# Band attention with a folded GLU: every head from 16 on transposed by VectorE and DMA, the first batch in plain fp32, and a fixed table of steps

## The chip, the cores and the metric

The kernel runs on one core of a Trainium2 chip. The metric is the time of one execution on the device in microseconds. The median of three runs of the kernel before is 893.46 us (892.77 to 895.96). Five engines run their own queues in order: TensorE (PE, with its weight loads PEld), VectorE (DVE), ScalarE (ACT), GpSimd (POOL) and SyncE (SP), which issues all DMAs here.

## The reference

Eight batches of eight heads, 512 local and 32 global tokens, 64 channels a head. Local queries see the global keys and a band of 32 local keys to each side; global queries see everything. The result goes through a bilinear GLU and two more matrices. All inputs are fp32 but the four weights, which arrive as 64-bit floats.

```python
def _attn_ref(q_l, k_l, v_l, q_g, k_g, v_g):          # B, H, Sl, D = 8, 8, 512, 64; Sg = 32
    k_all = np.concatenate([k_g, k_l], axis=2)
    v_all = np.concatenate([v_g, v_l], axis=2)
    s_g = scale * np.matmul(q_g, k_all.transpose(0, 1, 3, 2))
    out_g = np.matmul(sm(s_g), v_all)
    s_ll = scale * np.matmul(q_l, k_l.transpose(0, 1, 3, 2))
    mask = np.abs(pos[:, None] - pos[None, :]) <= 32
    s_ll = np.where(mask, s_ll, -1e9)
    s_lg = scale * np.matmul(q_l, k_g.transpose(0, 1, 3, 2))
    a_l = sm(np.concatenate([s_lg, s_ll], axis=-1))
    out_l = np.matmul(a_l, np.concatenate([v_g, v_l], axis=2))
    return np.concatenate([out_g, out_l], axis=2)

def _moe_ref(x, w1, w2, w3, w_out):                   # x: 4352 tokens x 512
    return ((x @ w1) * (x @ w2) @ w3) @ w_out
```

## The kernel before

**Precision.** Most matmuls take operands declared as `float32r`. So as to lose little precision the kernel splits an operand into a high part (a cast copy, `hi_of`, L308) and a low part (the operand minus its high part, `lo_of`, L311) and adds products of the parts. Local keys are held twice, on both halves of the partitions; of a head's queries the high part lies on one half and the low part on the other. So `kh` times both query parts and `kl` times both make four products in two instructions. P and V are split in the same way; the values come out on two halves of the partitions and are added (`values_half` copies one half to `cb`, `values_sum` adds it).

**A head** (64 of them, number n = 8 * batch + head). Loads of k, q and v; the casts and subtractions; `scores` (L386) on TensorE, four blocks of 128 queries with windows of 192 or 256 keys; `minus_max` (L398) on VectorE and `exps` (L402) on ScalarE write P into one of two tiles `Ps`; the inverse sums go through DRAM and come back spread over the partitions (`inverse_out`, `inverse_in`). P has to be transposed for the product with V. In most heads `transposes` (L448) does it with seven 128x128 transposes on TensorE into PSUM. In every second head from 16 on (`turned`, L30) `turn` (L427) transposes 32x32 blocks on VectorE, `turned_out` (L433) writes the blocks to DRAM and two edges within SBUF with six DMAs, and `turned_in` (L442) fetches them with two DMAs. In both cases `weights_hi` and `weights_lo` then write the parts of P transposed into `PTh`, `PTl` and `G` (global keys), from PSUM or from the P tile. There are six or seven such pieces a head: pieces 0 (own keys), 1 and 2 (the edges of the band), 3 and 6 (global keys), 4 and 5 (the global queries' weights). `values` (L506) multiplies; after two heads `join`, `normalize` and `convert` make the columns of x, and `join_g` adds up the outputs of the global queries in the tile `xg`.

**Global queries.** For each pair of heads `g_scores`, `g_half`, `g_minus_max`, and for each four heads `g_exps`, `g_normalize`, `g_transposes`, `g_weights`.

**Weights.** In the first stage the 64-bit words are unpacked to fp32 (`unit`), `fold` multiplies w3 by w_out once in plain fp32 (64 products of 512 columns), and the results are split (`fold_split`). Half of w1 and w2 comes in this stage, the rest (`w12s`) a little later.

**GLU.** `first` (L618) computes x times w1 and w2 for a quarter of the hidden units and 256 tokens, `gate_a` and `gate_b` multiply them, `second` (L647) multiplies by the folded matrix into two accumulators; after four quarters `evict` and `store`. There are 68 quarters, one for each head from head 8 on while heads last, and twelve after the last head, four of them for the global tokens.

**Order.** Everything is issued in an order that is computed while the kernel is built. Each step has a set of engines it may go to, a price on each (`COST`), a due time and the steps it needs. `list_schedule` (L129) walks through time: each engine that is free takes the available step with the earliest due time, moved by the numbers of `DUE`, `HEADS`, `UNITS` and `SUMS`. Steps that read SBUF on VectorE or GpSimd are priced as excluding each other. The engines' queues then hold the steps in the order of their starts.

## Time and profile before

| | before |
|---|---|
| median of 3 runs | 893.46 us (892.77 to 895.96) |
| profiled execution, its own time | 898.31 us |
| its span, first to last instruction | 896.5 us |
| mean granted TensorE clock | 0.978 |
| busy: PE, DVE, ACT, POOL | 832.8, 630.3, 616.4, 491.2 us |
| DMA: moved, mean rate | 103.38 MB, 115 GB/s |
| recorded DMA issues | 651, all from SP |

The page shows one execution. Its busy times are sums over the span; a group of instructions carries its line, engine, operation, tiles, shapes and count, then its busy time and the mean of one in ns, then the idle time of the engine before them and what ended it. Matmuls are pipelined, so their durations overlap and the time from one start to the next is the cost. In a table of waits the columns are the total in us, how often, and the longest. Heads can be counted by `u<-av,cb`, two for each head.

### The profile page before, as it was taken

Reading aid. Unit: us, or ns where it says so; the run is one execution under the profiler, and the core shown is the slowest. Engines: PE = TensorE matmul, PEld = TensorE weight load, DVE = VectorE, ACT = ScalarE, POOL = GpSimd, SP = SyncE. Lnnn points to the kernel's source line nnn. Section 1 sums busy time; section 2 is a strip of 40 time slices with the busy share of each in tenths; the row PEclk is TensorE's granted clock in tenths of the full one; section 3 lists DMA queues with packets and bytes.
Section 4 is the critical chain, followed back from the end, with each engine's and each line's share of the span. In section 5 each row is a group of like instructions: output and inputs, shape, how many; then the busy total and the mean of one; then the engine's idle time right before and its main releaser. Section 6 shows DMA issues by size and latency. Waiting matters only on the chain. (4 is left out here: it accounts for less than half of the span.)

```text
span 896.5 us, 17912 instructions
## 1 busy us (share of the span) xinstructions
PE 832.8 (93%) x5848; PEld 753.6 (84%) x5848; DVE 630.3 (70%) x1623; ACT 616.4 (69%) x1671; POOL 491.2 (55%) x592
## 2 busy tenths in 40 slices
PE   2788975999999999999999999999999999999995
PEld 1444645999989999999899989999999899999994
DVE  4888797888877878877787777778877798422111
ACT  4888777788878778787778777778777777312111
POOL 3455666566575767676668565857685656300000
PEclk9999876999999999999999999999999999999998
DMA  8786534424344435344535353436343522200000
GB/s 282 230 248 207 173 115 136 122 74 111 89 109 127 130 106 146 107 127 108 143 99 134 100 152 90 125 101 163 91 129 101 148 72 67 55 25 1 24 24 24
DMA packets 76917, 103.38 MB, mean 115 GB/s; under 512 B 20120, under 2 KB 38040, under 8 KB 76824
## 3 DMA queue, kind: packets, MB, share of 16 engines
q1 hardware_dynamic: 76824, 102.24, 40.8%
q8 instruction: 46, 0.75, 0.4%
q14 instruction: 47, 0.39, 0.2%
HBM read 84.71 MB, written 16.91 MB: 113 GB/s over the span
## 5 line engine op out<-in xcount | busy, mean ns | idle before, releaser
L627 PE MATMUL ap<-x,w12h 128*128 128x256 f32 x544 | 152.5, 280 | 2.1 <-ACT as__2970 L633 1.1
L627 PE MATMUL bp<-x,w12h 128*128 128x256 f32 x544 | 153.8, 283 | 0.0
L628 PE MATMUL bp<-x,w12h 128*128 128x256 f32 x544 | 152.0, 279 | 0.0
L629 PE MATMUL bp<-x,w12l 128*128 128x256 f32 x544 | 151.7, 279 | 0.0
L628 PE MATMUL ap<-x,w12h 128*128 128x256 f32 x544 | 151.0, 278 | 0.0
L629 PE MATMUL ap<-x,w12l 128*128 128x256 f32 x544 | 150.9, 277 | 0.0
L311 POOL TENSOR_TENSOR qs<-qr,qs 64x512 fp32r<-64x512 f32 x62 | 82.2, 1325 | 83.1 <-ACT qs L308 68.7
L403 ACT ACTIVATE P<-P,mn 128x192 f32<-128x192 f32 (+1 forms) x256 | 121.0, 474 | 2.8 <-DVE mn L399 1.9
L627 PEld LDWEIGHTS ap<-x,w12h 128*128 128x128 f32 x544 | 102.5, 188 | 4.1 <-ACT as__2970 L633 1.5
L628 PEld LDWEIGHTS bp<-x,w12h 128*128 128x128 f32 x544 | 103.2, 190 | 2.5
L627 PEld LDWEIGHTS bp<-x,w12h 128*128 128x128 f32 x544 | 103.3, 190 | 2.4
L628 PEld LDWEIGHTS ap<-x,w12h 128*128 128x128 f32 x544 | 102.3, 188 | 1.3 <-POOL x L311 0.2
L629 PEld LDWEIGHTS bp<-x,w12l 128*128 128x128 f32 x544 | 103.0, 189 | 0.0
L629 PEld LDWEIGHTS ap<-x,w12l 128*128 128x128 f32 x544 | 102.2, 188 | 0.0
L399 DVE CUSTOM_DVE_ANT_0 P<-s,cs 128x192 f32<-128x192 f32 (+1 forms) x256 | 86.9, 387 | 13.1 <-PE s L395 11.0
L532 DVE TENSOR_TENSOR u<-av,cb 64x352 f32<-64x352 f32 x128 | 65.0, 518 | 28.3 <-ACT cb L308 25.8
L308 ACT COPY cb<-av 64x352 f32<-64x352 f32 x127 | 56.6, 447 | 38.6 <-PE av L518 36.8
L395 PE MATMUL s<-kh,qs 128*128 128x192 f32 (+1 forms) x256 | 66.6, 292 | 17.0 <-DVE mg L569 7.0
L311 POOL TENSOR_TENSOR kl<-kr,kh 128x608 fp32r<-128x608 f32 x49 | 74.8, 1526 | 12.6 <-ACT kh L308 9.4
L764 PE MATMUL w<-wo,w3f 128*128 128x512 f32 x128 | 63.7, 645 | 10.8 <-DVE w3f L688 10.8
L395 PEld LDWEIGHTS s<-kh,qs 128*128 128x128 f32 x256 | 51.2, 200 | 22.4 <-DVE mg L569 8.8
L518 PE MATMUL av<-PTl,vs 128*128 128x192 f32 (+1 forms) x256 | 65.3, 280 | 3.9 <-DVE PTl L311 3.9
(800 smaller groups left out, 2399.7 us busy)
## 6 DMA issues: line engine op xcount, KB each, us to landing
kr<-in_kd_t_dram SPq DMA_DIRECT2D x128, 152.0 KB, 2.9
raw_w<-in_w_t_dram SPq DMA_DIRECT2D x24, 512.0 KB, 5.3
kpr<-in_kp_t_dram SPq DMA_DIRECT2D x32, 272.0 KB, 3.1
out_dram<-o SPq DMA_DIRECT2D x34, 256.0 KB, 3.0
vr<-in_v_t_dram SPq DMA_DIRECT2D x32, 256.0 KB, 2.9
qr<-in_q_t_dram SPq DMA_DIRECT2D x32, 256.0 KB, 3.5
R<-rd SPq DMA_DIRECT2D x64, 128.0 KB, 3.1
pd<-P SPq DMA_DIRECT2D x96, 80.0 KB, 1.9
```

The costliest lines, as they stand in the source:

```text
L308: (nc.scalar.copy if eng in (None, nc.scalar) else eng.tensor_copy)(dst, src)
L311: (eng or nc.gpsimd).tensor_sub(dst, src, f(hi))
L395: nc.tensor.matmul(st[:, e, 0:w], qs[:, 128 * e : 128 * e + 128], kk[:, o : o + w], start=(j == e % 2 == 0), stop=(j == 1), skip_group_che ...
L399: nc.vector.tensor_tensor_reduce(blk(n, e), cut(n, T["st", n][:, e, 0 : WIN[e][1]]), cut(n, masks[e]), -0.125, 3.0e38, ALU.add, ALU.min, T ...
L403: nc.scalar.activation(blk(n, e), blk(n, e), AF.Exp, bias=T["mn", n][:, e : e + 1], scale=-1.0, accum_out=T["sm", n][:, e : e + 1])
L518: nc.tensor.matmul(av[:, o : o + c1 - c0], v, pt[:, j, c0:c1], start=False, stop=(j % 2 == y == 1), skip_group_check=True)
L532: nc.vector.tensor_add(T["u", n // 2][r : r + 64, x], T.pop(("av", n, x))[r : r + 64, 0:352], T["cb", n][r : r + 64, x])
L627: nc.tensor.matmul(d, wh[:, k, c, :], x[:, 0, 0:w], start=(k == m % 2 == 0), stop=False, skip_group_check=True)
L628: nc.tensor.matmul(d, wh[:, k, c, :], x[:, 1, 0:w], start=False, stop=False, skip_group_check=True)
L629: nc.tensor.matmul(d, wl[:, k, c, :], x[:, 0, 0:w], start=False, stop=(k == 3), skip_group_check=True)
L764: nc.tensor.matmul(T["w34", t], T["w3f", t, j // 4][:, j % 4], T["wo"][:, j], start=(j == 0), stop=(j == 7))
```

## The change

- **Turned heads.** `TURN` goes from 2 to 1: all 48 heads from 16 on are turned by VectorE and DMA, where 24 were. `NPB` = 3 tiles of P replace two.
- **xg in DRAM.** The sums of the global queries leave SBUF: after each pair of heads one small DMA (`global_out`), and four loads (`global_in`) before the last quarters.
- **First batch in plain fp32** (`FS`, `FV` = 8). For heads 0 to 7 `scores` takes q and k as loaded, 64 rows each, in one fp32 product a block; `values` takes V as loaded, 32 or 128 rows, and P's transposed parts as fp32, with the output on 64 partitions. So there are no high and low parts of k, q, v and the global v, no low parts of P, no `cb`; `values_sum` is one copy from PSUM. k is loaded once, not twice, for these heads. `PTh`, `G` and `vgs` are declared again as float32r for head 8, and four clears of them (and of `PTl`) stand after the values of head 7.
- **Order.** `list_schedule` and its numbers are gone. `in_order` reads a table: for each step its rank among all 4218, with a letter for the engine (A, D, P for ScalarE, VectorE, GpSimd) where more than one is allowed.
- **More choice of engines.** Casts and copies that only ScalarE (or ScalarE and GpSimd) made may now go to VectorE: `hi`, `xh`, `cg`, `ga` among them. By the letters, over heads 16 to 63: the four turned pieces' high parts 122 on ScalarE, 35 on VectorE, 35 on GpSimd; their low parts 104 on VectorE, 88 on GpSimd; kl 26 and 22; ql 27 and 21; cb 75 on ScalarE, 21 on VectorE.

```diff
-TURN, FROM, AHEAD = 2, 16, 6.0
+TURN, FROM, AHEAD, NPB = 1, 16, 6.0, 3
+FS, FV = 8, 8
-DUE = dict(
...
+ORDER_OF = dict(
...
+    s="34 77 105 165 242 296 334 392 460 528 634 729 836 885 923 1020 1087 1133 1177 1273 1335 1388 1427 1531 1579 "
...
+    T="1123 1165 1212 1294 1370 1417 1462 1556 1609 1644 1718 1793 1866 1912 1952 2051 2104 2137 2212 2290 2362 2405 "
...
+    dr="1151 1189 1241 1323 1401 1445 1490 1581 1635 1669 1745 1817 1893 1942 1983 2082 2135 2161 2243 2315 2389 "
...
+    kl="P378 P480 D625 P657 P760 P852 P903 P958 P1032 P1101 D1173 P1213 D1307 P1345 D1414 P1458 P1542 D1593 D1686 "
...
-def list_schedule(steps, after, held):
...
+def in_order(steps, after, held):
+    words = {k: iter(v.split()) for k, v in ORDER_OF.items()}
+    letters, out = dict(A="ACT", D="DVE", P="POOL"), []
+    for n, (key, on, *_) in enumerate(steps):
+        word = next(words[key[0]])
+        out.append((int(word.lstrip("ADP")), n, letters[word[0]] if word[0] in letters else [*on][0]))
+    out.sort()
...
-    Ps = [const.tile([128, PW], F32, tag=f"P{e}", name=f"P{e}") for e in range(2)]
+    Ps = [const.tile([128, PW], F32, tag=f"P{e}", name=f"P{e}") for e in range(NPB)]
...
-    xg = const.tile([128, NP, TG], F32, tag="xg", name="xg")
+    xg = dram.tile([NP, 128, TG], F32, tag="xg", name="xg")
...
     def scores(n):
+        if n < FS:
+            r = 64 * (n % 2)
+            q, k = T["qr", n // 2][r : r + 64], T.pop(("kr", n))[r : r + 64]
+            for e in range(4):
+                o, w = WIN[e]
+                nc.tensor.matmul(st[:, e, 0:w], q[:, 128 * e : 128 * e + 128], k[:, o : o + w], start=(e % 2 == 0),
+                                 stop=True, skip_group_check=True)
+            return
...
     def values(n, x):
+        if n < FV:
+            nc.tensor.matmul(av[0:64, g0 : g0 + (256 if x else 288)], vgs[0:32, 0], G[0:32], start=True, stop=False,
+                             skip_group_check=True)
+            for j, o, c0, c1 in parts:
+                nc.tensor.matmul(av[0:64, o : o + c1 - c0], T["vr", n // 2][:, n % 2, j], W["PTh"][:, j, c0:c1],
+                                 start=False, stop=(j % 2 == 1), skip_group_check=True)
+            return
...
+    def values_sum(n, x, eng=None):
...
+        if n < FV:
+            hi_of(T["u", n // 2][r : r + 64, x], T.pop(("av", n, x))[0:64, 0:352], eng)
+            return
...
+    def global_out(m):
+        b, p = divmod(m, NP)
+        nc.sync.dma_start(xg[p, :, 32 * b : 32 * b + 32], T.pop(("gt", m))[:, 0])
+
+    def global_in(p):
+        T["xgr", p] = p2.tile([128, KD], F32, tag="kr", name=f"xgr{p}", bufs=NK)[:, 0:TG]
+        nc.sync.dma_start(T["xgr", p], xg[p])
...
-        return dict(ACT=(ns, False, 0), POOL=(170 + 1.2 * cols, True, HOLD_P))
+        return dict(ACT=(ns, False), DVE=(130 + 0.56 * cols, True), POOL=(170 + 1.2 * cols, True))
...
+    for key, name, ns in (("PTh", "PTh", 957), (1, "PTl", 962), (2, "G", 552), ("vgs", "vgs", 952)):
+        add(("clear", key), only("POOL", ns), base(FV) - 1.0, [("av", FV - 1, x) for x in range(2)], clear_weights, name, True)
...
-        for _, n, e in list_schedule(steps, after, held):
+        for _, n, e in in_order(steps, after, held):
```

More of the change, by code (lines that the diff above doesn't have):

```diff
@@ new lines, in in_order @@
+def in_order(steps, after, held):
[5 more added lines that the diff above has]
+    out.sort()
+    place = {steps[n][0]: r for r, n, _ in out}
+    assert all(place[k] < place[key] for key, ks in after.items() for k in ks)
+    return out
@@ L265, in clear, with clear_weights @@
         nc.gpsimd.memset(f(ap), 0.0)
+    def clear_weights(name, again):
+        if again:
+            weights_tile(name)
+        clear(W[name][64:128] if name in ("G", "vgs") else W[name])
     T = {}
@@ L461, in pieces @@
     def pieces(n, e):
+        PTh, PTl, G = W["PTh"], W.get("PTl", W["PTh"]), W["G"]
         def own(pt):
@@ L888, in head @@
             read(("s", n), h)
-        read(("s", n), ("kl", n))
-        add(("s", n), only("PE", COST["scores"]), t + 2.7, [("kl", n), ("ql", n)], scores, n)
+        if n >= FS:
+            read(("s", n), ("kl", n))
+        add(("s", n), only("PE", COST["scores" if n >= FS else "scores32"]), t + 2.7, [("kl", n), ("ql", n)] if n >= FS else [("load", "k", n), ("load", "q", n // 2)], scores, n)
         for e in range(4):
@@ L1089, in quarter @@
                 take("o", NO, ("o", k, e), me)
-                add(me, dict(ACT=(COST["out"], False, 0), DVE=(691, False, HOLD_A)), u + 2.5, [("second", k, 7, (e,) if last else None)],
+                add(me, dict(ACT=(COST["out"], False), DVE=(691, False)), u + 2.5, [("second", k, 7, (e,) if last else None)],
                     evict, key, w, e, eng=True)
```

414 lines of the change are left out of this document (221 added, 193 removed), and 137 rows, old and new, of tables (UNITS, av, cb, exps).

## The prediction

> **What bounds the kernel now.** I read the page's slices first, then the table of stretches, then the waits of the first stretch, then the rows of single instructions.
>
> ```profile
> PE 832.8 (93%) x5848; PEld 753.6 (84%) x5848; DVE 630.3 (70%) x1623; ACT 616.4 (69%) x1671; POOL 491.2 (55%) x592
> PE   2788975999999999999999999999999999999995
> ```
>
> TensorE is full from the eighth slice on; the first seven are another stage, with holes. The table of stretches, cut at the first matmul of the GLU (151.4) and at the last matmul (886.8), gives both their size (columns: length, busy time of each engine, granted clock, DMA share, GB/s):
>
> ```profile
> core 0: us, PE busy (x) PEld busy (x) DVE busy (x) ACT busy (x) POOL busy (x), PEclk, DMA share, GB/s
> 0.00:151.40 151.40, 105.65 (x391) 65.76 (x391) 117.04 (x286) 111.80 (x284) 78.22 (x96) 0.90 0.67 203
> 151.40:255.00 103.60, 101.77 (x771) 96.56 (x770) 85.53 (x235) 81.93 (x234) 64.13 (x78) 0.99 0.38 103
> 255.00:775.00 520.00, 513.63 (x3887) 487.00 (x3888) 402.93 (x1064) 400.46 (x1115) 343.76 (x413) 1.00 0.43 115
> 775.00:886.80 111.80, 111.78 (x803) 104.29 (x801) 24.83 (x38) 21.59 (x39) 5.08 (x7) 1.00 0.04 15
> 886.80:896.50 9.70, 0.00 (x0) 0.00 (x0) 0.00 (x0) 0.59 (x1) 0.00 (x0) 0.75 0.18 54
> ```
>
> So the span is 151.4 of a starved first stage, 735.4 in which TensorE idles 8.2, and 9.7 of last store. The first stage waits for the vector side:
>
> ```profile
> PE w L764 <- DVE w3f L688: 10.8, 2, 10.1
> PE s L395 <- DVE mg L569: 7.0, 2, 4.2
> PE sg L554 <- DVE mn L399: 5.4, 3, 2.7
> PE s L395 <- ACT TGg L599: 4.9, 1, 4.9
> ```
>
> There VectorE is busy 117.04 of 151.40 (77%), ScalarE 74%: that is what short dependent steps on strict queues reach. The change works on both stages, so I cost them apart.
>
> **First batch in plain fp32.** The two-row splits kh/kl, qh/ql, vh/vl, vgh/vgl, all lo steps of P and the cb copies go for heads 0 to 7; TensorE pays with fp32 passes. The weight fold is already plain fp32:
>
> ```profile
> 77.15 7.05 PE L764 MATMUL w<-wo,w3f 128*128 128x512 f32 x16
> 36.10 0.32 PE L513 MATMUL av<-G,vgs 128*128 128x288 f32 x1
> 37.25 3.62 PE L764 MATMUL w<-wo,w3f 128*128 128x512 f32 x8
> 560.22 0.90 PE s L395 x8
> ```
>
> Sixteen recorded instructions are eight products (64 products show as 128), so one product of 512 columns takes 7.05/8 = 0.88 us, 1.72 ns a column. Scores have 896 columns: 1.54 us against 0.90. Values have 544 for the global part and 832 for the local one, 1376: 2.37 us against 37.25 - 36.10 = 1.15. That is +1.86 a head, +14.9 for eight. If contracting over 64 or 32 rows made the passes cheaper it could be +0; I take 14.9, the row of the same type.
>
> What VectorE and ScalarE lose in this stretch (first 151.4 us, nine heads' rows):
>
> ```profile
> L311 DVE TENSOR_TENSOR PTl<-t,PTh 128x512 fp32r<-128x512 f32 x9 | 6.2, 691 | 2.2 <-ACT PTh L308 2.0
> L311 DVE TENSOR_TENSOR G<-t,G 32x384 fp32r<-32x384 f32 x9 | 5.0, 559 | 0.2
> L311 DVE TENSOR_TENSOR PTl<-t,PTh 32x96 fp32r<-32x96 f32 x18 | 4.5, 252 | 2.6 <-ACT PTh L308 1.2 <-ACT G L308 0.9
> L532 DVE TENSOR_TENSOR u<-av,cb 64x352 f32<-64x352 f32 x16 | 8.2, 520 | 1.2 <-ACT cb L308 1.0
> L308 DVE COPY cb<-av 64x352 f32<-64x352 f32 x1 | 0.5, 519 | 0.0
> L308 ACT CAST kh<-kr 128x608 fp32r<-128x608 f32 x10 | 6.9, 695 | 4.5 <-DMA kr<-in_kd_t_dram 1.8 <-issue 1.5 <-PE s L395 1.3
> L308 ACT COPY cb<-av 64x352 f32<-64x352 f32 x15 | 6.6, 447 | 1.2 <-PE av L518 0.8
> ```
>
> VectorE: 15.7 of lo for nine heads, 14 for eight; sums 8.2, of which the table leaves it 4 copies at 0.52. Against that it takes 13 of the high copies of these heads and three of w34h, about 5. Net 117 - 14 - 6 + 5 = 102; at the same 77% that is a stage of 132. ScalarE loses kh, 8 x 0.70, the q and v casts of about that size together, and cb, 6.6, and gets 12 sums at 0.45: about 97, at 74% a stage of 131. TensorE: 105.65 + 14.9 = 120.6 plus some 10 us before its first weights are unpacked: 131 if its clock stays as it is. The three agree, so I take **131**, 20.4 less. Below: TensorE at full clock. There its work to this point is 64 folds at 0.88, ten scores, nine transposes and eight values at the rows above, about 84, now 99; with 10 of start and some stalls 118. Above: 151, if the weights' arrival sets it. In the table TensorE has done the same work ahead of its first GLU matmul (all 64 folds, ten scores, nine groups of transposes), so what follows is comparable. Four clears now stand on GpSimd between the values of head 7 and those of head 8:
>
> ```profile
> L265 POOL MEMSET PTh<- 128x1024 f32 x1 | 1.0, 955 | 0.0
> ```
>
> Some 3.4 us with the half-size ones; folds lie on TensorE there, and without that cover they cost this once.
>
> The granted clock of this stage is 0.90 on average. The Trainium skill (TensorE: Matmul & The Clock Gate, What's actually happening) has the array at half clock after an idle window of about 3.4 us; the trace agrees, with gaps of 4.2 and 4.9 in the rows above and a clock of 0.90 against 1.00 later. By that rule fewer gaps give the full clock back and the stage would be 118, the sum 855; by the row it is 131.
>
> **Heads 16 to 63 all turned.** 24 more heads lose their seven transposes on TensorE (chain of waits, one head):
>
> ```profile
> 561.12 0.44 PE t L452 x4
> 561.55 0.33 PE t L455 x3
> L532 DVE TENSOR_TENSOR u<-av,cb 64x352 f32<-64x352 f32 x92 | 46.5, 518 | 24.1 <-ACT cb L308 22.1
> ```
>
> 0.77 a head, 18.5 in all. The stretch 255 to 775 holds 92/2 = 46 heads at 11.30 us; TensorE needs 513.63/46 = 11.17 of it and would need 11.17 - 0.385 = 10.78. That only counts if the others keep that pace. VectorE has 402.93/46 = 8.76 a head now. Added, by the letters of the table for heads 16 to 63 (D is VectorE) times rows of this case:
>
> ```profile
> 603.84 0.85 DVE L429 STREAM_TRANSPOSE P<-P 128x640 f32<-128x640 f32 x1
> 605.14 0.26 DVE L311 TENSOR_TENSOR PTl<-t,PTh 32x96 fp32r<-32x96 f32 x1
> L311 DVE TENSOR_TENSOR kl<-kr,kh 128x608 fp32r<-128x608 f32 x2 | 1.6, 792 | 2.0 <-ACT kh L308 2.0
> L311 DVE TENSOR_TENSOR qs<-qr,qs 64x512 fp32r<-64x512 f32 x2 | 1.4, 684 | 0.0
> L311 DVE TENSOR_TENSOR kpl<-kpr,kph 128x544 fp32r<-128x544 f32 x2 | 1.4, 718 | 1.0 <-ACT kph L308 1.0
> ```
>
> The turn itself, 605.14 - 603.84 = 1.30 for half the heads: +0.65. kl from 11 of 46 to 26 of 48: +0.24. ql from none to 27: +0.38. kpl from one to 13: +0.18. Copies that were ScalarE's or fixed (21 cb at 0.52, 40 of P's high parts at about 0.28, some 36 others at about 0.5, ten fewer evictions): about +0.6. A few more mul, xl and gl: +0.3. The lo steps, now from SBUF: -0.1, since GpSimd takes 88 of the 192. Sum 11.0 a head. So VectorE, not TensorE, would be the fuller engine, and 10.78 is out of reach if these prices hold. I take a pace of **11.2**: VectorE's 11.0 with almost no idling. That is 48 x 0.1 = 4.8 less than now: most of the 18.5 is lost again. Bounds: 10.85 (VectorE at fewer collisions) and 12.0 (below).
>
> The moved transfers: a turned head issues eight DMAs in a row, 24 heads 192 more, and the xg sums 36; the load of k in the first batch saves 8. SP has room, but in its order loads of k, q and v stand behind a dw that waits for T and a dr that waits for dw.
>
> ```profile
> pd<-P SPq DMA_DIRECT2D x96, 80.0 KB, 1.9
> P<-pd SPq DMA_DIRECT2D x24, 256.0 KB, 4.5
> ACT PTh L308 <- DMA P<-pd: 23.1, 16, 3.5
> PE av L518 <- DVE PTl L311: 0.9, 1, 0.9
> ```
>
> ScalarE already waits 23.1 for P<-pd over 24 heads, without TensorE waiting; the third P tile lets scores run a head further ahead. I put 0 on it, and a microsecond a head where that cover is gone. The sums of the global queries through DRAM are needed only in the last four quarters: 0, a few us if late. The last two stretches stay as they are.
>
> **Sum.** Span 896.5 - 20.4 - 4.8 = 871.3. The profiled execution took 898.31, and the median of the runs, 893.46, lies 3.0 under its span: 871.3 - 3.0 = **868**.
>
> **Rivals.**
> *TensorE stays the only bound* (pace 10.85, first stage 125): 896.5 - 26.4 - 21.6 - 3 = 846. For it: TensorE idled only 6.4 in 520 us so far. Against it: VectorE's 11.0.
> *The first stage gains nothing*, because weights arrive no sooner (DMA share 0.67, 203 GB/s there): stage 150, 896.5 - 1.4 - 4.8 - 3 = 887. Against it: the waits above name engines.
> *The turn through DRAM comes late*: half a microsecond at the values of each of 48 heads, 24 us: 892. For it: the landing of 4.5; against it: TensorE's values wait 0.9 in all between 255 and 775, the row above.
> *VectorE and GpSimd block each other* (slower). A subtraction with both inputs in SBUF is seen to wait for GpSimd:
>
> ```profile
> 603.12 0.18 DVE L538 TENSOR_TENSOR u<-u 128x32 f32<-128x32 f32 x1
> 623.11 1.38 DVE L538 TENSOR_TENSOR u<-u 128x32 f32<-128x32 f32 x1
> 623.10 1.34 POOL L311 TENSOR_TENSOR kpl<-kpr,kph 128x544 fp32r<-128x544 f32 x1
> L311 DVE TENSOR_TENSOR PTl<-P,PTh 32x96 fp32r<-32x96 f32 x19 | 18.4, 970 | 6.0 <-ACT PTh L308 4.7 <-DMA vgr<-in_vg_t_dram 1.1
> ```
>
> The same add takes 0.18 alone and 1.38 when GpSimd began a subtraction just before, to whose end it lasts; 32x96 takes 970 ns from SBUF and 252 from PSUM. The change moves four subtractions of 24 heads from PSUM to SBUF sources and adds about three such VectorE steps a head. If each waits a third of a microsecond, less than half of that 0.72, VectorE needs 12.0: 48 x 0.7 = 33.6 more, less 20.4: 896.5 + 13.2 - 3 = 907. It decides from a pace of 11.30 + 20.4/48 = 11.7. The Trainium skill (SBUF — State Buffer, SBUF: two separate sides) says so too: the shared port pair is an exclusive lock between GpSimd and a VectorE instruction with two SBUF inputs or in a two-port mode, so the new copies would take it as well; the trace agrees for the adds, and has too few such copies to tell.
>
> **Numbers.** Forecast 0.45 (own range 855 to 882), TensorE bound 0.17, no gain at the start 0.10, late turn 0.09, blocking 0.19. What a measurement tells from no change is 0.5%, 889.0 to 897.9. Faster: 0.45 + 0.17 + 0.06 + 0.03 = 0.71; same 0.04 + 0.05 = 0.09; slower 0.20. The range 845 to 900 leaves out part of the second and most of the last.
>
> **What would show it.** Right: the first GLU matmul near 131 and a granted clock above 0.90 before it; 16 groups of t; VectorE above 95% between heads 16 and 63; TensorE idling 0.3 to 0.5 a head there. Wrong: TensorE still at 99% (then 846), or values waiting for PTl from GpSimd or for P<-pd, or a first GLU matmul near 150.

## The result: slower by about half a per cent, and the profile after

The kernel after takes 899.08 us (median of 18 runs, 894.97 to 903.24), the kernel before, measured beside it, 893.68 us: a ratio of 1.0057, 95% interval 1.0041 to 1.0074. I had forecast 868 and faster. The time lies 0.9 us inside the upper end of the wide range (845 to 900) and outside my own (855 to 882), and the sign is wrong. The ratios here and below leave out executions that took clearly longer than the others of the same kernel: one of the six of the first reordered kernel (2112.26 us), and three of the ten (893.67 to 896.09) of the kernel after with less work for TensorE.

The first lines of the page of the kernel after (busy time of each engine, then the slices of TensorE and of its granted clock, then the shares of the chain that ended last):

```profile
span 896.2 us, 17663 instructions
...
PE 841.2 (94%) x5696; PEld 743.3 (83%) x5696; DVE 683.5 (76%) x1780; ACT 511.2 (57%) x1382; POOL 428.6 (48%) x628
...
PE   3999998899998979998999899998999899999995
...
PEclk9999999999999989999999999998999899999998
...
PE 72%; DVE 10%; DMA 6%; ACT 4%; issue 3%; SPq 2%; POOL 1%; DVEq 0%; ACTq 0%; POOLq 0%
```

The row of TensorE has changed places with the one of before. There the first seven slices had holes and all that followed was nines; here the start is full and the eights and sevens come back at even distances behind it, each some 94 us, the length of a batch. The clock's row has its eights at some of them. VectorE went up from 630.3 to 683.5 us and ScalarE down from 616.4 to 511.2: the letters of the table moved copies from one to the other, and the turn is VectorE's.

The same in stretches, cut at 129.2, where the kernel after starts its GLU (columns as in the prediction's table), first after:

```profile
0.00:129.20 129.20, 114.13 (x416) 62.16 (x417) 93.28 (x260) 79.95 (x212) 33.18 (x58) 1.00 0.74 210
129.20:255.00 125.80, 120.84 (x915) 114.66 (x914) 112.02 (x305) 87.78 (x246) 76.16 (x103) 0.99 0.47 125
255.00:775.00 520.00, 494.19 (x3563) 461.87 (x3562) 447.21 (x1162) 334.38 (x910) 302.19 (x447) 0.97 0.54 141
```

and before, the same cuts:

```profile
0.00:129.20 129.20, 94.43 (x341) 55.72 (x341) 100.04 (x239) 93.61 (x231) 66.08 (x80) 0.94 0.69 211
129.20:255.00 125.80, 112.99 (x819) 106.59 (x819) 102.53 (x283) 100.12 (x289) 76.28 (x94) 0.93 0.41 112
```

Up to 255 us the kernel after is well ahead: TensorE did 114.13 us of work where it had done 94.43, at the full clock. Between 255 and 775, where before idled 6.4 us at a clock of 1.00, it idles 520 - 494.19 = 25.8 us and the clock is 0.97. The lead melts batch by batch. Start of the first `ap` matmul of each batch in the two traces (every 64th of the 544 of its line, L627 before and L792 after):

| batch | 0 | 1 | 2 | 3 | 4 | 5 | 6 | 7 | span |
|---|---|---|---|---|---|---|---|---|---|
| before | 155.6 | 244.0 | 336.7 | 426.0 | 516.6 | 608.2 | 697.7 | 785.0 | 896.5 |
| after | 130.6 | 224.8 | 324.3 | 419.0 | 515.8 | 609.9 | 703.7 | 785.4 | 896.2 |
| lead | 25.0 | 19.2 | 12.4 | 7.0 | 0.8 | -1.7 | -6.0 | -0.4 | 0.3 |

From batch 2 to batch 6 a head takes (697.7 - 336.7)/32 = 11.28 us before and (703.7 - 324.3)/32 = 11.86 after. (The two spans are alike although the medians differ by 5.4: the profiled execution of before took 898.31, against its median of 893.46, and that of after 898.1, against 899.08.)

**Where the 25.8 us lie.** The waits of TensorE between 255 and 775 in the kernel after (total, times, longest):

```profile
PE av L670 <- DVE PTl__1085 L444: 3.9, 4, 1.5
PE av L665 <- ACT kh L441: 3.7, 1, 3.7
PE av L665 <- DVE G__1075 L444: 2.7, 3, 1.4
PE av L665 <- POOL G__1075 L444: 2.3, 2, 2.1
PE acc L822 <- ACT gh__6715 L441: 1.9, 1, 1.9
```

They are many, short, and of one place: the end of a batch. The timeline of TensorE at the first of them shows it. Head 23 is the last of its batch, and head 24 the first of the next; counted in order, the values (`av`) at 313.24 are head 23's and those from 321.52 on are head 24's (idle time and its releaser in brackets):

```profile
313.24 0.32 PE L665 MATMUL av<-G__1075,vgs__1059 128*128 128x288 f32 x1
...
315.07 0.50 PE L822 MATMUL acc<-w34h,gh__3914 128*128 128x512 f32 x1 [0.20 <-ACT gh__3914 L441]
315.41 0.40 PE L823 MATMUL acc<-w34l,gh__3914 128*128 128x512 f32 x1
316.86 0.51 PE L824 MATMUL acc<-w34h,gl__3940 128*128 128x512 f32 x1 [1.06 <-POOL gl__3940 L444]
...
319.06 0.39 PE L824 MATMUL acc<-w34h,gl__3940 128*128 128x512 f32 x1
321.52 0.40 PE L665 MATMUL av<-G__1075,vgs__1059 128*128 128x288 f32 x1 [2.07 <-POOL G__1075 L444]
321.75 0.25 PE L670 MATMUL av<-PTh__1052,vs 128*128 128x192 f32 x1
323.52 0.53 PE L670 MATMUL av<-PTl__1085,vs 128*128 128x192 f32 x1 [1.52 <-DVE PTl__1085 L444]
...
324.31 0.44 PE L792 MATMUL ap<-x,w12h 128*128 128x256 f32 x1
```

TensorE has run out of the old batch's GLU. It waits for the last gate parts of that batch, then for the weights of head 24, and only then comes the GLU of the new batch. What that GLU needs, x, is finished on ScalarE just before:

```profile
323.52 0.40 ACT L441 CAST x<-u 128x256 fp32r<-128x256 f32 x1
```

So at this end two chains run out together: head 23's, through its values to x, 0.4 us ahead of the GLU, and head 24's, whose values stand ahead of the GLU in TensorE's queue. Head 24 is one of those that the change turns; head 23 was turned in both kernels. The values of the next batch's first head stand ahead of its GLU at four of the five ends of after (not at 419.0), and the last cast of x ahead of it ends there 0.4 to 3.4 us before the GLU starts; in before, at the same place, head 24's values come at 338.05, behind the GLU's start at 336.69. Of TensorE's waits at the five ends, 18.9 of the 25.8 us, 9.9 are for these values and 9.0 for gate parts. From 322.9 on the record of the granted clock is 0.50 for 6.8 us; a stretch of two of them:

```profile
324.00:326.00 2.00, 2.00 (x11) 2.00 (x11) 1.13 (x5) 1.44 (x3) 0.00 (x0) 0.50 0.82 246
```

Such a hole stands at each of the five batch ends in this stretch, from 308.9, 406.1, 501.8, 594.8 and 688.7 on: 12.9 to 15.4 us without a matmul of `first`, partly filled with other work, where before has no such gap above 5.4. (The holes of the runs below are given in the same measure.) Behind each lie 3.4 or 6.8 us of half clock, 27.2 in all.

**Why the GLU ran out.** The chain from the end of the last head's scores to the first GLU matmul of the next batch is about as long in both kernels, 26.7 us before, 27.1 to 30.6 after. What differs is how TensorE is filled under it. First before, then after, two windows each from the end of such scores to the next batch's first GLU matmuls:

```profile
310.30:337.00 26.70, 26.70 (x199) 25.09 (x198) 20.85 (x66) 21.02 (x61) 16.54 (x20) 1.00 0.41 112
399.60:426.30 26.70, 26.70 (x199) 25.10 (x198) 20.20 (x66) 21.04 (x60) 17.05 (x22) 1.00 0.39 108
```

```profile
295.20:324.30 29.10, 24.26 (x160) 21.45 (x159) 23.45 (x68) 19.07 (x54) 20.07 (x25) 0.98 0.50 138
391.90:419.00 27.10, 24.77 (x156) 21.64 (x155) 20.61 (x65) 18.44 (x52) 16.38 (x18) 0.94 0.49 129
```

199 matmuls before, 160 and 156 after. The first line of `first` in the first windows, before and then after:

```profile
L627 PE MATMUL bp<-x,w12h 128*128 128x256 f32 x20 | 5.6, 279 | 0.0
...
L627 PE MATMUL ap<-x,w12h 128*128 128x256 f32 x17 | 4.7, 279 | 0.0
```

```profile
L792 PE MATMUL bp<-x,w12h 128*128 128x256 f32 x16 | 4.5, 284 | 0.0
...
L792 PE MATMUL ap<-x,w12h 128*128 128x256 f32 x8 | 2.2, 281 | 0.0
```

With the two other lines of `first`, 106 of its matmuls stand behind such scores at each of the five ends of before, and 70 to 72 at those of after. A step has twelve, so in the table of the kernel after the last head's scores stand three GLU steps later than the list scheduler had put them. The rest of the difference between 199 and 160 is in part the seven transposes of a head that before does not turn. And in the 60 us ahead of such scores VectorE has hardly a gap left, here the stretch before 391.9 after, and the one before 399.6 of before:

```profile
331.90:391.90 60.00, 59.35 (x451) 56.28 (x450) 55.96 (x133) 38.16 (x100) 36.27 (x55) 1.00 0.52 145
```

```profile
339.60:399.60 60.00, 60.00 (x460) 57.16 (x460) 46.83 (x120) 47.57 (x134) 42.07 (x51) 1.00 0.48 128
```

55.96 of 60 us against 46.83; over the five batch ends of after it is 50.5 to 56.0. In the 29.1 us of the first hole's window above it is 23.45, 81%.

### The profile page after: what moved, and what is told of

It reads as the page before. It is cut to its first block, busy times and chain, and to the rows that moved or that the text cites. A ratio compares the mean times of both kernels' runs of the same rounds, so it can differ in the third digit from the quotient of the medians.

```text
span 896.2 us, 17663 instructions
## 1 busy us (share of the span) xinstructions
PE 841.2 (94%) x5696; PEld 743.3 (83%) x5696; DVE 683.5 (76%) x1780; ACT 511.2 (57%) x1382; POOL 428.6 (48%) x628
## 4 chain that ended last, share of the span: by engine, by line
PE 72%; DVE 10%; DMA 6%; ACT 4%; issue 3%; SPq 2%; POOL 1%; DVEq 0%; ACTq 0%; POOLq 0%
PE w L929 6%; PE ap L792 6%; PE ap L793 6%; PE ap L794 6%; PE bp L792 5%; PE acc L824 5%; PE bp L794 5%; PE bp L793 5%; PE acc L823 5%; PE acc L822 5%; PE s L537 5%; PE av L670 4%; PE s L530 2%; DMA P<-pd 2%; PE sg L719 2%
## 5 line engine op out<-in xcount | busy, mean ns | idle before, releaser
L792 PE MATMUL ap<-x,w12h 128*128 128x256 f32 x544 | 154.5, 284 | 0.0
L793 PE MATMUL ap<-x,w12h 128*128 128x256 f32 x544 | 153.2, 282 | 0.0
L794 PE MATMUL ap<-x,w12l 128*128 128x256 f32 x544 | 153.1, 281 | 0.0
L792 PE MATMUL bp<-x,w12h 128*128 128x256 f32 x544 | 152.7, 281 | 0.0
L792 PEld LDWEIGHTS ap<-x,w12h 128*128 128x128 f32 x544 | 104.9, 193 | 1.6
L793 PEld LDWEIGHTS ap<-x,w12h 128*128 128x128 f32 x544 | 104.2, 192 | 1.5
L792 PEld LDWEIGHTS bp<-x,w12h 128*128 128x128 f32 x544 | 102.8, 189 | 0.9
L444 POOL TENSOR_TENSOR PTl__1085<-P,PTh__1052 32x96 fp32r<-32x96 f32 (+1 forms) x78 | 51.5, 661 | 33.6 <-DVE PTh__1052 L441 8.9
L687 DVE TENSOR_TENSOR u<-av,cb 64x352 f32<-64x352 f32 x112 | 56.2, 518 | 10.3 <-ACT cb L441 7.9
L441 ACT COPY cb<-av 64x352 f32<-64x352 f32 x88 | 38.7, 448 | 42.9 <-PE av L670 36.9
L670 PE MATMUL av<-PTl__1085,vs 128*128 128x192 f32 x224 | 58.7, 286 | 4.0 <-DVE PTl__1085 L444 3.9
L537 PE MATMUL s<-kh,qs 128*128 128x192 f32 x224 | 56.9, 286 | 5.1 <-DVE mg L734 3.9
L929 PE MATMUL w<-wo,w3f 128*128 128x512 f32 x128 | 61.0, 610 | 0.0
L537 PE MATMUL s<-kl,qs 128*128 128x192 f32 x224 | 56.7, 287 | 0.5 <-DVE kl L444 0.5
L670 PE MATMUL av<-PTh__1052,vs 128*128 128x192 f32 x224 | 55.7, 271 | 0.0
```

The costliest lines, as they stand in the source:

```text
L444: (eng or nc.gpsimd).tensor_sub(dst, src, f(hi))
L537: nc.tensor.matmul(st[:, e, 0:w], qs[:, 128 * e : 128 * e + 128], kk[:, o : o + w], start=(j == e % 2 == 0), stop=(j == 1), skip_group_che ...
L670: nc.tensor.matmul(av[:, o : o + c1 - c0], v, pt[:, j, c0:c1], start=False, stop=(j % 2 == y == 1), skip_group_check=True)
L687: nc.vector.tensor_add(T["u", n // 2][r : r + 64, x], T.pop(("av", n, x))[r : r + 64, 0:352], T["cb", n][r : r + 64, x])
L792: nc.tensor.matmul(d, wh[:, k, c, :], x[:, 0, 0:w], start=(k == m % 2 == 0), stop=False, skip_group_check=True)
L793: nc.tensor.matmul(d, wh[:, k, c, :], x[:, 1, 0:w], start=False, stop=False, skip_group_check=True)
```

## The experiments

The questions, in order: which of the two parts costs, is it the order of the table, is it VectorE's work or the trip through DRAM, is it the half clock, and what does TensorE's relief bring. In the expectations D stands for the delay that the turn adds to the last head of a batch, V for VectorE's work, O for the order.

**The trip through DRAM taken away.** The four writes of P's blocks and the two reads are left out, so P's pieces are read where they lie and the values are others; all else stays.

```diff
     def turned_out(n):
...
-        for x in range(4):
-            nc.sync.dma_start(d[:, :, x].rearrange("s p w -> p s w"),
-                              P[32 * x : 32 * x + 32, 128:768].rearrange("p (s w) -> p s w", s=5))
...
     def turned_in(n):
...
-        nc.sync.dma_start(P[:, 256:768], d[1:5].rearrange("s p x w -> (s p) (x w)"))
-        nc.sync.dma_start(spread(n, [256]), d[0].rearrange("p (a b) w -> p a (b w)", b=2))
```

> Edit: the changed kernel, table and all, without the trip of the turned weights through DRAM (the four writes of P into pd and the two reads back are left out, so the weights of heads 16 to 63 stand in the wrong places; the transposes on VectorE and the two small moves inside P stay). The changed kernel measured 899 us. Theory D (the turned weights come late at the end of each batch, and TensorE runs dry for it): the 8 us between the end of the turn and the landing of P fall out of the chain, the holes of 13 to 15 us between GLU matmuls shrink, the time falls by 12 to 25, to 874 to 887. Theory O (the written-out order itself leaves TensorE without GLU matmuls once a batch, whatever the transfers do): holes of 12 us and more stay, 893 to 899. Theory V (VectorE's 10.2 us of work a head set the pace): no change of VectorE's work, 895 to 899.

888.6 us, 0.9938 of before (0.9918 to 0.9958), 10.5 under the kernel after: just above what D expected, clearly below O. The holes stay, 9.7 to 15.4 us, and a head takes 11.58. In the trace of the kernel after the transposes of head 24 end at 309.65, its writes are issued until 313.94, its reads from 314.75, and P has landed at 318.09: 8.4 us. So taking some 8 us out of every turned head's chain is worth 0.22 us a head and closes no hole. The edit takes the trip from all 48 heads, while the change had added it to 24 of them, so 10.5 is not what the change's own trips cost; the kernel before without its trips was not run.

**The two large VectorE transposes taken away**, the trip kept; P is again not transposed.

```diff
     def turn(n):
         g = grid(n)
-        nc.vector.transpose(g[:, 1:6], g[:, 1:6])
-        nc.vector.transpose(g[:, 0:8:7], g[:, 0:8:7])
         nc.vector.transpose(g[:, 1, 0], g[:, 6, 0])
```

> Edit: the changed kernel without the two large transposes on VectorE (1.24 of the turn's 1.40 us a head; the small one stays, the DMAs stay, the weights of heads 16 to 63 stand in the wrong places). Theory V (VectorE is what sets the pace of heads 16 to 63): 48 x 1.24 = 60 us of VectorE's work less, and with VectorE over 90% busy between the holes a large part of it shows: 860 to 875. Theory D (the chain of the turn is late): each batch's chain is 1.2 us shorter, 7 holes, 885 to 892. Theory O: 890 to 899, since the sequence of TensorE's matmuls is the same and VectorE was not what it waited for for long.

883.68 us, 0.9893 (0.9876 to 0.9911), 15.4 under the kernel after, a head at 11.57; the holes are 11.7 to 14.4 us. Between V and D, and nearer to D. Here too all 48 heads are relieved, not only the 24 new ones. The 1.24 us a head by which this shortens the chain (839 + 400 ns, rows further down) is little against the 8.4 of the trip, and it brought more: microsecond for microsecond, VectorE's time counts for more than the delay.

**The kernel after in another order**, the same steps on the same engines; the ranks come from a search with a model of the queues.

```diff
 ORDER_OF = dict(
...
-    s="34 77 105 165 242 296 334 392 460 528 634 729 836 885 923 1020 1087 1133 1177 1273 1335 1388 1427 1531 1579 "
+    s="27 70 98 152 219 274 305 385 451 520 636 735 832 876 928 1020 1076 1121 1176 1261 1322 1378 1420 1518 1572 "
```

> Edit: the changed kernel with the same steps on the same engines, every engine letter of the table kept, only the ranks of the table changed (each step moved by 15 places of 4218 on average), so that the GLU matmuls of a batch last until the next batch's inputs are there. Theory O: the holes between GLU matmuls fall from 13 to 15 us to under 7, no half clock after 255 us, pace of heads 16 to 63 from 11.82 to 11.2 us or less: 865 to 880. Theory V (VectorE's load, 10.2 us a head, with its waits on GpSimd): the order cannot take work off VectorE, 890 to 905. Theory D (transfers late): as long as the chain through DRAM is the same length the stall comes back somewhere else, 888 to 900.

901.9 us, 1.0094 (1.0073 to 1.0116): no better than the table it replaces. Four of the five batch ends keep a hole of 11 to 14 us. The fifth has 5.4, and it is the only one where the search had put more GLU behind the last head's scores: 84 matmuls of `first`, against 58 to 70 at the others. So this order hardly tried a longer cover, and neither do the other reordered tables below, with 70 to 72.

**The control: the kernel before in an order of the same search**, the list scheduler replaced by a table in the manner of `in_order`.

```diff
+ORDER_OF = dict(
...
+    s="53 106 147 231 355 429 478 590 648 728 789 899 961 1007 1059 1141 1184 1231 1300 1365 1431 1469 1500 1615 "
...
-        for _, n, e in list_schedule(steps, after, held):
+        for _, n, e in in_order(steps, after, held):
```

> Edit: the kernel before with the same steps on the same engines in another written-out order, found in the same way as that of the run before this one: the control for it, to tell what a new order is worth without the change's parts. If a new order is worth as much here, the gain says nothing of the change. The profile of before has TensorE idle 8.2 us after the first GLU matmul, so the later stages can gain no more than that; the first stage (151.4 us) may gain some. Theory O: 880 to 892, against 865 to 880 for the changed kernel reordered. If the first stage can be packed by order alone as well as by the fp32 batch: 870 to 875.

924.25 us, 1.0345 (1.032 to 1.0369). The search made a good order worse. Its batch ends keep 106 to 119 matmuls of `first` behind the last head's scores and no gap above 5.5 us, so its loss lies elsewhere. A table that it finds and that is slow therefore says little about what could be had, and the run above leaves O open.

**The fp32 first batch alone.** The kernel after with every second head turned, two P tiles and `xg` in SBUF; up to 128 us the order of after, then that of before.

```diff
-TURN, FROM, AHEAD, NPB = 1, 16, 6.0, 3
+TURN, FROM, AHEAD, NPB = 2, 16, 6.0, 2
...
-    xg = dram.tile([NP, 128, TG], F32, tag="xg", name="xg")
+    xg = const.tile([128, NP, TG], F32, tag="xg", name="xg")
...
-    s="34 77 105 165 242 296 334 392 460 528 634 729 836 885 923 1020 1087 1133 1177 1273 1335 1388 1427 1531 1579 "
+    s="33 76 108 167 246 295 338 391 462 529 696 781 859 924 961 1033 1080 1119 1189 1267 1334 1368 1417 1517 1572 "
```

> Edit: the first part of the change alone. Heads 0 to 7 in plain fp32 (scores and values, one k load, the four clears), every other head turned or not as before (TURN 2, two P tiles, the xg sums in SBUF). The written-out order takes what starts in the first 128 us from the changed kernel's table with its engine letters, and everything later from the order and the engines of the kernel before. My theory (the first stage's gain is real and stands by itself; the loss comes with the turned heads and their order after it): first GLU matmul of a quarter near 131 us instead of 155.8, after it the pace of before, 11.30 us a head: 893.6 - 25 = 866 to 873. Rival (the stages are not independent: what the first stage gains is lost again as weights, loads of k, or the first batch's x come too late for the pace of before): 882 to 893.

893.67 us, 0.9997 (0.9983 to 1.0011). The first `ap` matmul of the GLU starts at 132.6, 23.0 us sooner than before, and 18 of them are gone at once. The time is that of before, 0.7 above the rival's range, and my theory's 866 to 873 is missed by 20. The longest wait of TensorE between 129 and 255 in this run:

```profile
PE ap L779 <- ACT as__1308 L438: 17.9, 1, 17.9
```

At the seam of the two orders ScalarE's queue had small steps on w1 and w2, waiting for their transfers, ahead of the copy of the gate. That is the seam's doing, not the first batch's, as the run with the seam mended shows further down. From 331.9 to 691.4 a head takes 11.23, as before.

**The turned part alone.** The kernel after without the fp32 first batch; up to 153 us the order of before, then that of after, 25 us later.

```diff
-FS, FV = 8, 8
+FS, FV = 0, 0
...
-    for name in ("PTh", "G", "vgs"):
-        weights_tile(name, False)
+    for name in ("PTh", "PTl", "G", "vgs"):
+        weights_tile(name)
```

> Edit: the other part alone. All heads from 16 on turned, three P tiles, the xg sums through DRAM, free copy engines, in the order and on the engines of the changed kernel's table; the first batch split into fp32r pairs as before, and what starts in the first 153 us in the order of the kernel before. My theory (the two parts add up): the first stage of before, 151 to 156 us, and the slower pace of the changed kernel, 11.8 us a head: 893.6 + 5.5 + 22 to 25, 916 to 924. Rival (the loss after the first stage is a consequence of the earlier start, since weights, loads and GLU inputs then collide with heads 8 to 20): 893 to 905.

913.35 us, 1.0221 (1.0199 to 1.0243): 19.5 us slower than before, a little less than my theory's 916 to 924. The stretch of heads in this run,

```profile
255.00:775.00 520.00, 496.29 (x3608) 464.20 (x3607) 452.51 (x1169) 337.95 (x915) 303.74 (x452) 0.98 0.52 142
```

is that of the kernel after, with holes of 12.8 to 15.4 us at the same five batch ends and 11.82 us a head. The loss belongs to the turned part as a whole, its order and engines included, and it stays when the first stage is that of before.

**The fp32 first batch alone, seam mended**: the same kernel, with the order of after kept up to 215 us.

```diff
-    s="33 76 108 167 246 295 338 391 462 529 696 781 859 924 961 1033 1080 1119 1189 1267 1334 1368 1417 1517 1572 "
+    s="33 76 108 167 246 295 338 391 462 529 631 724 832 878 917 1015 1079 1119 1189 1267 1334 1368 1417 1517 1572 "
```

> As the run with the fp32 first batch alone (every second head turned, two P tiles, the sums of the global queries in SBUF), but the order of the kernel after is kept up to 215 us and the order of before starts there, so that the small steps on w1 and w2 no longer stand ahead of a gate copy on ScalarE. Theory G (the first stage's gain of 22 us is real and stays, and the hole of 18.2 us at the seam ate it): first GLU matmul near 132, no hole over 6 us behind it, 864 to 876. Rival (the second stage gives the gain back whatever its order, because heads cannot be started earlier): 886 to 894, with TensorE idle somewhere between 132 and 300.

878.94 us, 0.9828 (0.9812 to 0.9843): faster than before and after, just above what G expected. From its page, and its stretch of heads:

```profile
PE 846.0 (96%) x5864; PEld 752.3 (86%) x5864; DVE 613.3 (70%) x1619; ACT 579.0 (66%) x1584; POOL 447.9 (51%) x562
...
PE   3999999899999999999999999999999999999995
```

```profile
255.00:775.00 520.00, 520.00 (x3929) 493.91 (x3928) 397.21 (x1045) 392.35 (x1089) 333.95 (x403) 1.00 0.41 111
```

TensorE is busy for all of 520 us at full clock; it waits nowhere in this stretch. At each of its five batch ends 106 matmuls of `first` stand behind the last head's scores, as in before, and no gap between matmuls of `first` is above 4.5 us. With it the two parts add up: -1.72% and +2.21% of before are +0.49%, where both together measured +0.57%.

**The kernel after in an order of a second search**, whose model has VectorE and GpSimd excluding each other and TensorE slow behind a hole; the engines stay.

```diff
-    s="34 77 105 165 242 296 334 392 460 528 634 729 836 885 923 1020 1087 1133 1177 1273 1335 1388 1427 1531 1579 "
+    s="34 75 98 149 221 282 309 389 457 520 632 729 828 883 915 1015 1087 1126 1171 1267 1331 1385 1427 1518 1575 "
```

> The kernel after with the same steps on the same engines, in an order of its steps found by a second search that counts VectorE and GpSimd as excluding each other when both read SBUF and TensorE as slow behind a hole. Theory O (the holes at the batch ends are a matter of the order alone): two or more of the five holes fall under 6 us and the time is 875 to 889. Theory D (with every head turned, the last head of a batch cannot be finished in time on these engines whatever the order): holes of 10 to 15 us stay at four or five batch ends, 893 to 905.

907.97 us, 1.0173 (1.0139 to 1.0208), holes of 11.5 to 14.5 us at all five ends.

**The same search, free to choose engines** (768 of 4218 steps change theirs; letters A, D, P in the table).

```diff
-    cb="D612 A617 A685 A693 A813 A814 A883 A886 D944 A948 D994 A998 A1060 A1065 A1125 A1132 A1223 D1228 A1248 A1251 "
+    cb="A611 A618 A685 D696 A798 A812 A878 A880 D941 A944 D986 A992 A1053 D1056 A1121 A1127 A1206 A1227 A1237 D1247 "
```

> The kernel after with an order of the same second search, which was also free to choose the engine of each step among those that the kernel allows (768 of 4218 steps change engine). Theory O: holes under 6 us at two or more batch ends, 870 to 887. Theory D: holes stay at four or five batch ends, 893 to 905. If this one closes the holes and the run with the engines kept does not, what binds is how the vector work is spread over the three engines.

905.68 us, 1.0135 (1.0101 to 1.0169), holes of 11.9 to 16.8 us at all five. Both lie a little above what D expected; after the control neither can carry a "whatever the order".

**Trip and transposes both taken away**: the two edits further up in one kernel.

> The kernel after without the two large VectorE transposes of each turned head and without the four writes to DRAM and the two reads from it (P's pieces are then P not transposed, so the values are others; every other step and the order stay). Alone, the one gave 15.4 us and the other 10.5. Theory D (what the turn adds between a head's scores and its values makes the holes at the batch ends, and VectorE's load with it): the two add up, 868 to 878, and three or more of the five holes fall under 8 us. Rival O (the table puts the last head's scores so late on TensorE that a hole stays whatever the steps cost): 880 to 889, holes of 10 us or more at four or five batch ends.

877.39 us, 0.9832 (0.9801 to 0.9862), 21.7 under the kernel after. The time is D's: the two nearly add up (10.5 + 15.4 = 25.9). The holes are O's: 9.3 to 14.6 us at all five ends, a head at 11.54. So even with nothing of the turn left but the small transpose, the two small moves within P and their places in the queues, this order does not come near the 10.9 that TensorE's work asks for. Its stretch of heads:

```profile
255.00:775.00 520.00, 503.63 (x3680) 473.84 (x3679) 419.58 (x1091) 334.51 (x911) 308.62 (x457) 0.98 0.33 86
```

**More for TensorE near the hole**: idle products ahead of the values of a batch's last head, overwritten at once.

```diff
+        if x == 0 and n in (23, 31, 39, 47, 55):
+            w = T["vs", n // 2][:, n % 2]
+            for y in range(18):
+                nc.tensor.matmul(av[:, 0:256], w[:, 0].rearrange("p a b -> p (a b)"), w[:, 0:2].rearrange("p j a b -> p (j a b)"),
+                                 start=True, stop=True, skip_group_check=True)
```

> The kernel after with 18 idle matmuls of 256 columns (about 2.1 us at full clock) on TensorE ahead of the first value matmul of heads 23, 31, 39, 47 and 55; their output is written over at once. The records of the kernel after have 27.2 us at half clock at the batch ends, which is 13.6 us of lost work. Theory H (the half clock is a loss of its own): the half clock goes at three or more of the five ends and the time falls by 6 to 14 us, 885 to 893. Rival (the head's chain on the other engines sets when the next batch begins, and a faster TensorE only waits longer): 896 to 904.

900.9 us, 1.009 (1.0049 to 1.0132), no different from the kernel after. The half clock fell from 27.2 to 20.4 us in this stretch of the record and went from one batch end of five, so the loss by the clock itself was not isolated. Nor did the products fill a wait: they ran at 316.66, 2.33 us long, ahead of head 23's values, where TensorE has no wait in the kernel after, and the waits for head 24's values stayed behind them, 2.29 and 1.51 us. The run tells neither H from its rival nor what the waits cost.

**Less work for TensorE, in the kernel after**: the products with the low part of k are left out for heads 16 to 63 (kl is still made, the scores are less precise).

```diff
         for e in range(4):
             o, w = WIN[e]
-            for j, kk in enumerate((kh, kl)):
+            for j, kk in enumerate((kh, kl)[: 1 + (n < 16)]):
                 nc.tensor.matmul(st[:, e, 0:w], qs[:, 128 * e : 128 * e + 128], kk[:, o : o + w],
-                                 start=(j == e % 2 == 0), stop=(j == 1), skip_group_check=True)
+                                 start=(j == e % 2 == 0), stop=(j == int(n < 16)), skip_group_check=True)
```

> The kernel after without the products with the low part of k in the scores of heads 16 to 63 (half of the scores' matmuls; kl is still made): 0.45 us less of TensorE a head, 21.6 in all. Theory V (with all heads turned the vector engines and the chain through DRAM set the pace of the heads): 892 to 901, and TensorE idles more. Rival T (TensorE sets the pace, and only the order leaves holes in it): 876 to 883.

889.57 us, 0.9937 (0.9905 to 0.9969), 9.5 under the kernel after by the medians and 10.7 by the ratios to before. That is 44 to 50% of the 21.6 us taken from TensorE: more than V allowed, less than T asked for.

**The same relief, in the kernel of the fp32 first batch with the mended seam.**

> The kernel of the fp32 first batch with the mended seam, with the same products with the low part of k left out (kl is still made). There TensorE is busy all of 255 to 775. Theory T (with every second head turned TensorE alone sets the pace): most of 21.6 us goes, 857 to 866. Theory V extended (the vector engines stand just behind TensorE in this order too, so that a relief of TensorE is worth little whoever gives it): 870 to 879, with holes at the batch ends.

862.57 us, 0.9665 (0.9637 to 0.9692), 16.4 under 878.94, or 14.6 by the ratios to before: 68 to 76% of 21.6, with no hole at any batch end and a head at 10.89, as T expected. Its stretch of heads:

```profile
255.00:775.00 520.00, 514.72 (x3856) 485.90 (x3855) 397.33 (x1045) 392.31 (x1089) 334.10 (x400) 1.00 0.41 112
```

Here TensorE, busy for 514.72 of 520 us, does set the pace, and what it is spared is kept for the most part. The kernel after kept a smaller share of it, but the two kernels were measured on different chips and the intervals of the two gains overlap, so that the relief is worth more here is indicated, not shown.

What the edits brought in the kernel after, beside what they took out:

| taken from the kernel after | gained |
|---|---|
| 8 us of each turned head's chain (trip) | 10.5 |
| 60 us of VectorE (48 x 1.24) | 15.4 |
| both | 21.7 |
| 21.6 us of TensorE | 9.5 to 10.7 |

No edit gave back all that it took out of an engine, so neither engine is the bound alone. I read that as a kernel in which TensorE, VectorE and the chains at the batch ends take turns on the way to the end; no run shows the turns themselves.

## Why the prediction failed, step by step

**First stage, 131: right, 129.2 measured, in part by luck.** The sums of TensorE, VectorE and ScalarE had agreed on 131, but VectorE did 93.28 us of work instead of 102 and ScalarE 79.95 instead of 97, so by their shares the stage would have been shorter; and two terms of TensorE were off and cancelled. The fp32 passes cost more than the 14.9 us I took from the fold's 1.72 ns a column. Scores of one head, then the values of one head, in the timeline of the kernel after (start, duration, both halves of the values up to the next fold):

```profile
87.43 1.78 PE L530 MATMUL s<-kr,qr 64*128 64x192 f32 x8
89.14 1.98 PE L929 MATMUL w<-wo,w3f 128*128 128x512 f32 x4
```

```profile
102.42 0.69 PE L659 MATMUL av<-G,vgs 32*64 32x288 f32 x2
103.05 0.92 PE L662 MATMUL av<-PTh,vr 128*64 128x192 f32 x4
103.89 0.64 PE L659 MATMUL av<-G,vgs 32*64 32x256 f32 x2
104.46 0.92 PE L662 MATMUL av<-PTh,vr 128*64 128x224 f32 x4
105.31 1.12 PE L929 MATMUL w<-wo,w3f 128*128 128x512 f32 x2
```

Scores 89.14 - 87.43 = 1.71 us (1.54 predicted), values 105.31 - 102.42 = 2.89 (2.37): 2.55 a head more than the 0.90 and 1.15 of the split products, so 20.4 us for eight heads. Contracting over 32 or 64 rows made no column cheaper: the scores' 896 columns took 1.91 ns each, the values' 1376 took 2.10, against the fold's 1.72. What made up for it was the clock, 1.00 instead of 0.94 up to 129.2, and shorter waits; the longest of TensorE in this stage:

```profile
PE sg L719 <- DVE QG L444: 9.1, 1, 9.1
PE t L594 <- ACT P L545: 1.8, 1, 1.8
```

The Trainium skill (TensorE: Matmul & The Clock Gate, What's actually happening) has activity give the full clock back; the trace agrees, with 1.00 in the row of this stretch, though not for its start, where the same scores took 3.35 us at 11.78 and 1.78 at 24.46. The stage did not come to the 118 of that case either. Of the 11 us between, 20.4 - 14.9 = 5.5 are the fp32 products. QG's wait is the start itself, 9.1 us before the first matmul, which the 118 had as 10; the rest was not taken apart. With the mended seam the first batch alone is worth 15 us of the 20.4 forecast, and the rival that saw no gain in it falls.

**Heads 16 to 63 at 11.2: this is the step that failed; 11.86 measured (520/44 heads = 11.82 in the stretch).** I added up VectorE's work a head, got 11.0 and took it for the pace. VectorE does 447.21/44 = 10.16 us a head, so it was sized 0.84 too high, and still the heads are slower than either engine's work: TensorE needs (494.19 - 13.6 lost at half clock)/44 = 10.9. To that come 25.8/44 = 0.59 of idle time and 13.6/44 = 0.31 of half clock, and the three make the 11.8. The 0.66 us by which the pace missed, times 48 heads, is 31.7 us, and the time missed by 899 - 868 = 31: if that pace holds for all 48, this one term is the whole miss. The error is in the step from VectorE's sum to the pace, "VectorE's 11.0 with almost no idling". VectorE was not the bound that this makes it: it is busy 447.21 of 520 (86%), not above 95% as I had named for a sign. And TensorE, which should have idled 0.3 to 0.5 a head, idled 0.59, in holes at the batch ends that no term of mine had, and ran at half clock behind them; its values waited for PTl and G, near the sign of being wrong that I had named (PTl from GpSimd; the rows above have PTl from VectorE and G from GpSimd and VectorE).

That the holes come with the second part of the change (the turned heads, xg in DRAM, the freer choice of engines and the order of them) is shown by the run with the turned part alone. Why they open is indicated only. In the order of after, 70 to 72 matmuls of `first` stand under a chain of some 27 us where 106 did, and the next batch's first head, newly turned, has its values ahead of that batch's GLU. In every run with 106 or more there is no gap above 5.5 us and with 58 to 72 there is always a hole of 9 or more, but the runs with 106 also turn only every second head. The one end with 84 and a gap of 5.4 is the only sight of the cover apart from that. I had asked nowhere whether the GLU left in the queue covers that chain. It was there to be read: 106 in the trace of before, and in the table of after only six steps of `first` between the last head's scores and the next batch.

**Which terms of VectorE were off.** The turn costs (36.9 + 17.6 + 7.4)/44 = 1.41 us, 1.30 predicted, from these rows of the stretch 255 to 775; the subtractions of 32x96 from SBUF, 970 ns before, are 442:

```profile
L571 DVE STREAM_TRANSPOSE P<-P 128x640 f32<-128x640 f32 x44 | 36.9, 839 | 7.7 <-ACT P L545 7.1
...
L444 DVE TENSOR_TENSOR PTl__1085<-P,PTh__1052 32x96 fp32r<-32x96 f32 x27 | 11.9, 442 | 0.6
...
L572 DVE STREAM_TRANSPOSE P<-P 128x256 f32<-128x256 f32 x44 | 17.6, 400 | 0.0
...
L573 DVE STREAM_TRANSPOSE P<-P 128x32 f32<-128x32 f32 x44 | 7.4, 167 | 0.0
```

The copies and eviction steps that I put at 0.6 I did not take apart again.

**VectorE and GpSimd block each other: near in time, wrong in mechanism.** The rival's pace was 12.0 and its point of decision 11.7, so the measured 11.86 lies on its side, and its 907 is not far from 899. But its price, a third of a microsecond on each new subtraction on top of 252 ns, would make some 585 ns; the row shows 442, and 970 in before. Adding up by how much each VectorE step of the stretch is longer than the 10th percentile of its form gives 51 us after and 60 before, 1.17 and 1.31 us a head, when steps are grouped by line, operation and shapes: what is there has not grown. That the table keeps the two engines apart better than the scheduler had is my reading of it.

**The turn through DRAM at nothing: wrong by 0.22 us a head**, 10.5 us in all by the run without the trip, which takes it from all 48 heads; what the 24 new trips cost was not measured. I had named the cover, values that wait 0.9 us in all between 255 and 775, and read it as room; it was room of the old order. The rival "the turn comes late" had half a microsecond a head and the right place, TensorE's values waiting for PTl and G, but its 24 us is more than twice what the trip is worth. SP's queue stands before the turned heads' writes too, the first row of its waits in this stretch:

```profile
SPq L579 <- DVE P L573: 86.0, 39, 5.5
```

39 times it stands up to 5.5 us there, with the loads of later heads behind. That this costs time is not shown: in before the like row is 27.6, 15, 6.4, and yet all of SP's waits in this stretch together went down, from 278.5 to 176.5 us.

**TensorE stays the only bound, 846:** not in this kernel. It is nearly so with every second head turned.

**What remains open.** Whether any order of these steps closes the holes. The kernel after, the turned part alone and three other orders have them, but those orders come from a search that also spoiled the kernel before, and but for one batch end they leave no more GLU behind the last head's scores than the kernel after; at that end, with 84 matmuls, the hole was gone. That the last head's scores stand three GLU steps later is read from the trace. That moving them would help, or putting the values of the next batch's first head behind its first GLU steps, was not tried by itself. And the share of the half clock by itself stays unknown.

## What to carry to other kernels

Before work is moved off the fullest engine, look for the place where that engine runs out of filler, and compare the filler with the chain that it covers: here 106 matmuls of the GLU's first product had become 70 to 72 behind the last head of each batch, and no average of busy time shows it. Here the pace was not the largest of the engines' sums, with two of them at 86% and 92% on strict queues, and the relief of one came back only in part. And test the parts of a change apart: one of these two was worth 15 us, and the other cost 20.

## What the chip showed that I had not expected

The clock fell to half although TensorE never waited longer than 2.07 us at a time in the first hole: four waits, 0.20, 1.06, 2.07 and 1.52 us between 315 and 323.5, stood around the start of 6.8 us at 0.50 (from 322.9). And a small fp32 product took more a column than a large one here: the values' 1376 columns took 2.89 us, 2.10 ns each, where sixteen recorded folds took 7.05 us for eight products of 512, 1.72 ns.
